# Sharing one block of channels, moving a layer norm to ScalarE and holding back stores in a transformer block on one Trainium2 core

## The chip, the cores and the metric

The kernel runs on one core of one Trainium2 chip. The core has a matrix engine (TensorE, PE in the profile, with its weight loads shown as PEld), a vector engine (VectorE, DVE), an engine for activations (ScalarE, ACT), a general one (GpSimd, POOL) and one that only issues transfers (SyncE, SP). Each takes its instructions in a fixed order. Transfers run on 16 DMA engines. The metric is device time in microseconds (us) of one execution, lower is better.

## The reference

One block on x of 2048 positions and 576 channels, all tensors in bf16:

```
h  = x + A(layernorm(x))          # A: 32 heads of 18 channels; each position attends to 8 positions,
                                  #    2 apart (itself and 7 before it), then a product with wo
h2 = h + B(layernorm(h))          # B: layernorm once more, gelu(y @ w1 + b1) @ w2 + b2, 4608 hidden
```

In A, q, k and v come from one product with wqkv (576 x 1728). Scores are the sum of q times k over the 18 channels, followed by a softmax over the 8 positions. In B the two layer norms in a row are computed as one, with an adjusted epsilon.

## The kernel before, in words

**Tiles.** The positions are cut into 16 tiles j of 128 rows. Position 16p + j is row p of tile j, so the neighbours two apart lie in the same row of tile j - 2, and only the first tiles of each parity need rows shifted by one; these shifted copies of K and V (halos) go through a tensor in DRAM, kv_dram. `store_halo` writes K and V of a tile there, `halo(j, t)` reads one back into the ring buffer kv_ring. There are 15 stores in all. Attention goes over the even tiles from 14 down to 0, then over the odd ones from 15 to 1. `GROUPS` are pairs in that order: (14, 12), (10, 8), (6, 4), (2, 0), (15, 13) and so on. `A` is the same order as a list, so A[0] is tile 14, A[1] tile 12, A[2] tile 10.

**The contraction of 576 rows.** 576 is four and a half times 128. TensorE works here with two half arrays of 64 rows. One bank half (g = 0 or 1) is fed by the upper or the lower 64 rows, and then they swap: `phase(duo, 0, ...)` runs five blocks, `phase(duo, 1, ...)` four, each with two matmuls of 64 rows, so nine in all for each of the two outputs. The product with wqkv uses a fifth block that holds channels 448 to 575, with a swap of blocks 3 and 4 for one of the outputs (`if g == 0 and kt == KF - 1 and sl.start: kt = KF`). The products with wo and w1 use a fifth block that holds channels 512 to 575 twice, once in each half of the partitions. For that, `dma_out` writes the tile's 576 columns and then columns 512 to 575 once more to DRAM, from where a transposing DMA reads the tile back with channels on partitions. `transpose_in` does the same on TensorE, with two more small products when `twice` is set.

**Visits.** The first stage computes q, k and v in 24 visits, numbered 0 to 23. A visit is a set of two or three `duos`; all first phases run, then for each duo the second phase, followed by its eviction (`evac`) and the functions in `between`. Between the phases of a duo a no-operation on GpSimd (`marker`) tells TensorE that a half is free. The table `after` gives what is recorded behind a visit, `loads` which weights are loaded then, `hooks` what TensorE transposes between first and second phases, and `wo_with` puts the output projection of A[0] into visit 17 and that of A[1] into visit 19. The bank "D" serves the transposes and these projections in turn. Three other banks ("C", "A", "B") go round among the q, k, v products.

**LN2.** `ln2_h` adds the projection to x on VectorE. There are two ways from there: `ln2` and `ln2_more` with statistics on VectorE, `ln2_rstd` on GpSimd, `ln2_bias` on VectorE and `ln2_hn` on ScalarE; or `ln2_act` with mean, squares and scale on ScalarE and the root on GpSimd, followed by `ln2_send`. Tiles A[0] and A[1] go the first way.

**Rounds.** After the first stage, round k = 0 to 7 treats the pair GROUPS[k] (w1, gelu, w2) on TensorE, while VectorE does the attention of the next pairs. In the listing c, d are the tiles of GROUPS[k + 1] and e, f those of GROUPS[k + 2]. `m1` and `mid` hold what is recorded with the visits of the product with w1, `ia` and `ib` what is recorded within the products with w2 of the pair's first and second tile. The attention output goes to DRAM by `send_o` and comes back transposed by `read_o`; `wo_duo` uses it. `pending_halo` is the list of stores of K and V not yet made; `halos(n)` makes the next n of them, seven of these in round 1.

**Order.** The program runs under a manual schedule: each engine executes in the order in which the code records, and SyncE's transfers are issued in that order as well. A transfer that waits for something holds up all that SyncE issues behind it. The weight loads also wait for the latest eviction recorded at their place (`pace`).

Of the kernel before, what the change touches and what calls it, by code (L numbers as in the profile page):

```python
# [17 lines left out]
def kernel(  # L18
# [12 lines left out]
    nc = tc.nc  # L31
# [87 lines left out]
    def load_wo(qs):  # L119
        src = A_wo.rearrange("(h d) c -> h d c", h=H)  # L120
        for q in qs:
            load(wo_sb[q * H:(q + 1) * H, :, :], src[:, q:4 * KF:4, :])
            load(woh_sb[q * H:(q + 1) * H, :], src[:, 4 * KF + q % 2, q // 2 * HALF:(q // 2 + 1) * HALF])

    def load_w1h():
        load(b1_bf[:], B_b1.rearrange("(ft p) -> ft p", p=P))
        src = B_w1[KF * P:D, :].rearrange("p (u g c) -> p u g c", u=NU // 3, g=2)
        for r in range(2):
            load(w1h_sb[half_rows(r), :].rearrange("p (u c) -> p u c", u=NU // 3), src[:, :, r, :])

    def load_w1(c):
        cols = slice(c * F // 6, (c + 1) * F // 6)
        load(w1_sb[:, :, cols], B_w1[0:KF * P, cols].rearrange("(k p) c -> p k c", p=P))

    def load_w2(c):
        f0, f1 = (0, 4, 7, 11, 14, 21, FA, FT)[c:c + 2]
        dst = w2a_sb[:, f0:f1, :] if f1 <= FA else w2b_sb[:]
        load(dst, B_w2[f0 * P:f1 * P, :].rearrange("(ft p) c -> p ft c", p=P))
# [38 lines left out]
    def transpose_in(pair, src, twice=True):  # L177
        def turn(rows, kt, c):
            for r in range(2):
                block = src[half_rows(r), c:c + P if rows.start is None else D]  # L180
                nc.tensor.matmul(pair[rows, r, kt * HP:(kt + 1) * HP], lhsT=block, rhs=ident[half_rows(r), half_rows(r)],
                                 start=True, stop=True, skip_group_check=True)

        for kt in range(KT):
            turn(slice(None), kt, min(kt * P, D - P))
        if twice:
            turn(half_rows(0), KF, KF * P)
# [8 lines left out]
    def dma_out(src):  # L196
        td = dram.tile([P, KT * P], BF16, tag="td", name="td", bufs=4)
        nc.sync.dma_start(out=td[:, 0:D], in_=src)
        stored[0] = nc.sync.dma_start(out=td[:, D:KT * P], in_=src[:, KF * P:D]).ins
        return td  # L200
# [5 lines left out]
    def half_rows(r):  # L206
        return slice(r * HP, (r + 1) * HP)

# [51 lines left out]
    def tr_x(j, tag):  # L260
        pair = psum_pair(tag or "CAB"[(ring_pos[0] + 1) % 3], "xt_pt")
        transpose_in(pair, q_all[:, j, :], False)
        if EVEN.index(j) % 2 == 0:
            new_xnT(EVEN[EVEN.index(j):][:2])
        for k0, k1 in ((0, 2), (2, KT)) if j in EVEN[0:2] else ((0, KT),):
            copy = nc.vector.tensor_copy if j == EVEN[1] and k0 == 0 else nc.scalar.copy
            copy(**turned(xnT[j], pair, k0, k1))
# [21 lines left out]
    def store_halo(j, ts=slice(0, 2)):  # L289
        nc.sync.dma_start(out=kv_dram[j, 1:P + 1, ts, :], in_=kv_ring[j % 2][:, j // 2, ts, :])  # L290

    def qkv_duo(j, t):
        def make():
# [3 lines left out]
            def op(g, i, sl, kt):  # L297
                c0 = g * HALF
                if g == 0 and kt == KF - 1 and sl.start:
                    kt = KF  # L300
                return xt[sl, kt, :], (wq_sb[sl, kt, t * D + c0:t * D + c0 + HALF] if kt < KF else wqh_sb[sl, t, c0:c0 + HALF])
# [125 lines left out]

    def read_o(j):
        nc.sync.dma_start_transpose(out=new_oT(j)[:], in_=o_sent.pop(j)[:])
# [3 lines left out]
    def wo_duo(j, tag):  # L433
        def make():
# [3 lines left out]
            def op(g, i, sl, kt):  # L438
                c0 = g * HALF
                return t[sl, kt, :], (wo_sb[sl, kt, c0:c0 + HALF] if kt < KF else woh_sb[sl, :])  # L440
# [29 lines left out]
    def ln2_act(j):  # L470
        h = h_of[j]
        y = sb.tile([P, D], BF16, tag="hn", name="hn", bufs=2)
        nmean, var, rstd = (sb.tile([P, 1], F32, tag=f"ln2_{t}", name=f"ln2_{t}", bufs=2) for t in ("nmean", "var", "rstd"))
        nc.scalar.activation(out=y[:], in_=h[:], func=ACT.Identity, scale=-1.0 / D, accum_out=nmean[:])
        nc.scalar.activation(out=y[:], in_=h[:], func=ACT.Square, bias=nmean[:], accum_out=var[:])
        nc.scalar.activation(out=var[:], in_=var[:], func=ACT.Identity, scale=(1.0 + EPS) / D, bias=eps2[:])
        ins = nc.gpsimd.tensor_tensor(out=rstd[:], in0=var[:], in1=mhalf[:], op=ALU.pow).ins  # L477
        root[0] = ins if j not in GROUPS[1] else None
        hn[j] = (h, rstd, nmean, y)

    def ln2_send(j):
# [3 lines left out]
        hn[j] = dma_out(y[:])  # L485
# [56 lines left out]
    def mlp1_duo(grp, us, tag):  # L542
        def make():
# [5 lines left out]
            def op(g, i, sl, kt):  # L549
                f0 = fts[g][i] * P  # L550
                c0 = (GF * us[i // GF] + i % GF) * P
                return (w1_sb[sl, kt, f0:f0 + P] if kt < KF else w1h_sb[sl, c0:c0 + P]), ht[sl, kt, 0:N]
# [225 lines left out]
    with tc.manual_schedule(engines={ENG.PE, ENG.Activation, ENG.DVE, ENG.SP, ENG.Pool}):  # L778
# [144 lines left out]
        for n, v in enumerate((19, 19, 20, 20, 21, 22)):  # L923
# [18 lines left out]
            17: [c_(ln2, A[0]), c_(att_qk_a, A[2])],  # L942
            18: [c_(ln2_rstd, A[0]), c_(add_b2, A[0]), c_(ln2_bias, A[0]), c_(halo, A[2], 1), c_(att_qk_add, A[2], ((0, 0, 9),))],
# [6 lines left out]
            18: {1: [c_(tr_o, A[1], "D")]},  # L950
            19: [c_(ln2_hn, A[0])],
# [46 lines left out]
        def halos(n):  # L998
            for _ in range(min(n, len(pending_halo))):
                store_halo(pending_halo.pop(0))  # L1000
# [12 lines left out]
        for k, g in enumerate(GROUPS):  # L1013
# [11 lines left out]
            if k == 0:  # L1025
                m1[0] += [c_(halos, 1), c_(load_w2, 6), c_(att_qk_a, d), c_(att_qk_rest, d, 1), c_(halo, d, 1)]
# [7 lines left out]
                ib[8] = [c_(read_o, e), c_(out_store, g[0])]  # L1034
            elif k == 1:
                m1[0] += [c_(pv_sum, d), c_(send_o, d)]
                m1[1] += [c_(att_qk_a, e), c_(halo, e, 1), c_(read_o, d), c_(att_qk_b, e, 0), c_(halos, 7)]
                m1[3] += [c_(att_qk_a, f), c_(halo, f, 1), c_(att_qk_add, f, ((0, 0, 9), (0, 0, 4)))]
# [98 lines left out]
```

## Time and profile before

| | us |
|---|---|
| median of 3 runs | 362.56 (362.54 to 363.0) |
| the profiled execution, its own time | 366.0 |
| span of that execution, first to last instruction | 364.2 |
| first stage (q, k, v), until the first product with w1 | to 67.5 |
| round 0, round 1 (start of w1) | 67.5, 106.2 |
| round 2, 3, 4, 5, 6, 7 (start of w1) | 147.9, 184.4, 220.2, 256.0, 291.8, 327.3 |
| ScalarE busy, VectorE busy, of the span | 235.3, 296.6 |
| DMA, mean over the span | 127 GB/s |

The profile is one execution. Its page gives the busy time of each engine, the granted clock of TensorE, the waits and the costliest groups of instructions by line of the program. In the timeline a row gives the start, the length, the engine, the line, the operation, the tiles written and read, how often, and in brackets the engine's idle time before the row and what ended it. SPq marks SyncE's queue; the length there is that of the issue, not of the transfer.

### The profile page before, as it was taken

Reading aid. Unit: us, or ns where it says so; the run is one execution under the profiler, and the core shown is the slowest. Engines: PE = TensorE matmul, PEld = TensorE weight load, DVE = VectorE, ACT = ScalarE, POOL = GpSimd, SP = SyncE. Lnnn points to the kernel's source line nnn. Section 1 sums busy time; section 2 is a strip of 40 time slices with the busy share of each in tenths; the row PEclk is TensorE's granted clock in tenths of the full one; section 3 lists DMA queues with packets and bytes.
Section 4 is the critical chain, followed back from the end, with each engine's and each line's share of the span. In section 5 each row is a group of like instructions: output and inputs, shape, how many; then the busy total and the mean of one; then the engine's idle time right before and its main releaser. Section 6 shows DMA issues by size and latency. Waiting matters only on the chain.

```text
span 364.2 us, 11562 instructions
## 1 busy us (share of the span) xinstructions
PE 355.0 (97%) x4942; PEld 292.8 (80%) x4942; DVE 296.6 (81%) x417; ACT 235.3 (65%) x521; POOL 45.5 (13%) x61
## 2 busy tenths in 40 slices
PE   7999999999999799999999999999999999999996
PEld 3778977887789777887788778877887788778874
DVE  5999999999989889994799989989998998520431
ACT  4879756897637782468846956695669566805630
POOL 2240004000112010100020102020202020210000
PEclk9999999999999989999999999999999999999999
DMA  7986799963447584651283466344545354263001
GB/s 247 329 278 191 197 218 306 373 227 72 143 90 110 174 207 71 114 90 39 74 121 81 62 133 93 90 98 122 86 88 65 93 85 58 52 120 51 4 1 32
DMA packets 62980, 46.29 MB, mean 127 GB/s; under 512 B 32192, under 2 KB 60736, under 8 KB 62928
## 3 DMA queue, kind: packets, MB, share of 16 engines
q1 hardware_dynamic: 58960, 41.50, 43.2%
q0 software_dynamic: 3744, 3.84, 9.9%
q8 instruction: 38, 0.62, 0.7%
q10 hardware_dynamic: 224, 0.22, 0.2%
q14 instruction: 14, 0.11, 0.1%
HBM read 23.38 MB, written 12.42 MB: 98 GB/s over the span
## 4 chain that ended last, share of the span: by engine, by line
PE 79%; DVE 11%; DMA 6%; ACT 2%; issue 1%; POOL 0%; ACTq 0%; SPq 0%; POOLq 0%
PE pm L216 33%; PE po L664 25%; PE po L576 9%; PE pq L216 7%; PE pw L216 4%; DVE ln_stats L148 2%; DMA x_all<-in_A_x_dram 2%; DMA oT<-td 2%; DVE prod L393 1%; DMA xnT<-xd 1%; DVE prod L399 1%; DVE prod L347 1%; ACT h_all L557 1%; DVE ln_mv L149 1%; DVE prod L338 1%
## 5 line engine op out<-in xcount | busy, mean ns | idle before, releaser
L216 PE MATMUL pm<-hnT,w_sb 64*128 64x256 bf16 x2304 | 143.0, 269 | 0.0
L557 ACT ACTIVATE h_all<-pm,b_sb 128x256 f16<-128x256 f32 (+1 forms) x288 | 108.6, 496 | 51.0 <-PE pm L216 50.4
L216 PEld LDWEIGHTS <-w_sb 64*128 64x128 bf16 x2304 | 113.5, 94 | 13.4 <-issue 1.7
L664 PEld LDWEIGHTS <-h_all 128*128 128x128 f16 x480 | 46.2, 98 | 13.7 <-issue 1.6
L216 PE MATMUL pq<-wq_sb,xnT 64*128 64x288 bf16 x720 | 54.7, 283 | 1.1 <-ACT kv_ring L306 0.4
L216 PEld LDWEIGHTS <-xnT 64*128 64x128 bf16 x864 | 44.0, 94 | 9.9 <-issue 0.8
L347 DVE TENSOR_TENSOR prod<-prod 128x2304 bf16<-128x2304 bf16 (+1 forms) x64 | 44.2, 691 | 2.0
L338 DVE TENSOR_TENSOR prod<-kv_ring,q_all 128x4608 bf16<-128x4608 bf16 x16 | 40.9, 2556 | 3.2 <-POOL ln_rstd L477 2.5
L393 DVE TENSOR_TENSOR prod<-kv_ring,probs 128x4608 bf16<-128x4608 bf16 x16 | 40.9, 2558 | 0.8 <-DMA kv_ring<-kv_dram 0.3
L216 PE MATMUL pm<-hnT,w1h_sb 64*128 64x256 bf16 x288 | 39.5, 269 | 0.0
L664 PE MATMUL po<-w2a_sb,h_all 128*128 128x288 bf16 (+1 forms) x262 | 35.8, 286 | 0.0
L576 PEld LDWEIGHTS <-h_all 128*128 128x128 bf16 x288 | 28.3, 99 | 8.7 <-issue 1.2
L399 DVE TENSOR_TENSOR prod<-prod 128x2304 bf16<-128x2304 bf16 (+1 forms) x32 | 33.9, 1058 | 1.1
L664 PEld LDWEIGHTS <-kv_ring 128*128 128x128 f16 x252 | 24.6, 98 | 6.3
L576 PE MATMUL po<-w2a_sb,h_all 128*128 128x288 bf16 x224 | 29.6, 293 | 0.0
L216 PE MATMUL pq<-wqh_sb,xnT 64*128 64x288 bf16 x144 | 27.6, 283 | 0.0
L766 POOL DMA_DIRECT2D x_all<-o_sb x12 | 10.7, 890 | 126.1 <-PE pw L216 72.2
L216 PE MATMUL pw<-wo_sb,oT 64*128 64x288 bf16 x256 | 20.1, 288 | 2.4 <-DMA oT<-td 2.3
L644 DVE TENSOR_TENSOR kv_ring<-h_all 128x1536 f16<-128x1536 f16 (+3 forms) x9 | 6.8, 760 | 16.1 <-ACT h_all L557 16.1
L664 PE MATMUL po<-w2b_sb,h_all 128*128 128x288 bf16 (+1 forms) x122 | 19.7, 286 | 0.1
L216 PEld LDWEIGHTS <-oT 64*128 64x128 bf16 x288 | 13.8, 95 | 7.0 <-DMA oT<-td 3.3
L161 POOL TENSOR_TENSOR ln_rstd<-ln_veps,mhalf 128x1 f32<-128x1 f32 (+2 forms) x14 | 13.3, 964 | 48.5 <-DVE ln_veps L155 31.7
(107 smaller groups left out, 394.9 us busy)
## 6 DMA issues: line engine op xcount, KB each, us to landing
w_sb<-in_B_w_dram SPq DMA_DIRECT2D x6, 768.0 KB, 5.8
kv_ring<-kv_dram SPq DMA_DIRECT2D x28, 144.0 KB, 2.3
kv_dram<-kv_ring SPq DMA_DIRECT2D x13, 288.0 KB, 3.9
x_all<-in_B_b_dram SPq DMA_DIRECT2D x15, 144.0 KB, 3.7
w2a_sb<-in_B_w_dram SPq DMA_DIRECT2D x2, 1008.0 KB, 7.4
td<-q_all SPq DMA_DIRECT2D x14, 144.0 KB, 1.8
td<-hn SPq DMA_DIRECT2D x14, 144.0 KB, 1.8
x_all<-h POOLq DMA_DIRECT2D x14, 144.0 KB, 4.6
```

Source lines behind the costliest of these rows:

```text
L148: nc.vector.bn_stats(out=stats[:, i, c, :], in_=src[:, c * HALF:(c + 1) * HALF])
L161: nc.gpsimd.tensor_tensor(out=rstd[:], in0=veps[:], in1=mhalf[:].to_broadcast([P, n]), op=ALU.pow)
L216: last = nc.tensor.matmul(duo["g"][r ^ swap][i], lhsT=lhsT, rhs=rhs, start=(swap == 0 and i == 0 and kt == 0), stop=(swap == 1 and kt == K ...
L338: ins = nc.vector.tensor_tensor(out=prod[:], in0=k_ring[j % 2], in1=q_all[:, j, :].unsqueeze(1) .to_broadcast([P, W, D]), op=ALU.mult).ins
L347: nc.vector.tensor_tensor(out=prod[:, :, o * H:o * H + n], in0=prod[:, :, a * H:a * H + n], in1=prod[:, :, c * H:c * H + n], op=ALU.add)
L393: nc.vector.tensor_tensor(out=prod[:].rearrange("p w (d h) -> p w d h", h=H), in0=v_ring[j % 2].rearrange("p w (d h) -> p w d h", h=H), in ...
L399: nc.vector.tensor_tensor(out=prod[:, 0:n, :], in0=prod[:, 0:n, :], in1=prod[:, n:2 * n, :], op=ALU.add)
L557: pace[0] = nc.scalar.activation(out=hT(grp)[:, f, 0:N], in_=ps[:, r, i * N:(i + 1) * N], func=ACT.Gelu_apprx_tanh, bias=b1_sb[:, f:f + 1] ...
L576: nc.tensor.matmul(banks[half], lhsT=hT(grp)[:, f, i * P:(i + 1) * P], rhs=w2_rows(f)[:, half * HALF:(half + 1) * HALF], start=(f == 0), s ...
L644: nc.vector.tensor_tensor(out=s_slot(t, m0, m1), in0=a, in1=b, op=alu)
L664: nc.tensor.matmul(bank, lhsT=l, rhs=r, start=start, stop=stop, skip_group_check=True)
L766: nc.gpsimd.dma_start(out=x_of(j), in_=o_of.pop(j), accum_op=ALU.add)
```

## The change

Three things are changed.

*Shared channels.* The fifth block of o, of wo, of LN2's output and of w1 now holds channels 448 to 575, as that of wqkv does. The swap of blocks is put into a function `block`. `dma_out` writes columns 0 to 511 and then 448 to 575; `transpose_in` loses the `twice` products. The loads of wo and w1 are rearranged to match, and with them the number of transfers; the first six loads of w2 become four.

*LN2 of A[0].* It goes the ScalarE way, in three pieces: `ln2_mean` behind visit 17, `ln2_root` behind the first eviction of visit 18, `ln2_norm` behind the first eviction of visit 19.

*Transfers of rounds 0 and 1.* The output store of GROUPS[0][0] moves from round 0's second product with w2 to behind the seven stores of K and V in round 1. The load of V for d is recorded behind the store of o of d. Stores of K and V made after a read of o wait until the latest such read has landed.

```diff
 def load_wo(qs):
-            load(wo_sb[q * H:(q + 1) * H, :, :], src[:, q:4 * KF:4, :])
-            load(woh_sb[q * H:(q + 1) * H, :], src[:, 4 * KF + q % 2, q // 2 * HALF:(q // 2 + 1) * HALF])
+            rows, k = slice(q * H, (q + 1) * H), KF - q // 2
+            load(wo_sb[rows, 0:k, :], src[:, q:4 * k:4, :])
+            if q >= 2:
+                load(wo_sb[rows, k, 0:HALF], src[:, q + 4 * k + 2, 0:HALF])
+                load(wo_sb[rows, k, HALF:D], src[:, q + 4 * k, HALF:D])
+            load(woh_sb[rows, :], src[:, 4 * KF - 2 + q, q // 2 * HALF:(q // 2 + 1) * HALF])
 def load_w1(c):
-        load(w1_sb[:, :, cols], B_w1[0:KF * P, cols].rearrange("(k p) c -> p k c", p=P))
+        n = KF - 1 if c % 2 == 0 else KF
+        load(w1_sb[:, 0:n, cols], B_w1[0:n * P, cols].rearrange("(k p) c -> p k c", p=P))
+        for r in range(2 * (KF - n)):
+            load(w1_sb[half_rows(r), n, cols], B_w1[n * P + 2 * r * HP:n * P + 2 * r * HP + HP, cols])
 def load_w2(c):
-        f0, f1 = (0, 4, 7, 11, 14, 21, FA, FT)[c:c + 2]
+        f0, f1 = (0, 7, 14, 21, FA, FT)[c:c + 2]
 def dma_out(src):
-        nc.sync.dma_start(out=td[:, 0:D], in_=src)
-        stored[0] = nc.sync.dma_start(out=td[:, D:KT * P], in_=src[:, KF * P:D]).ins
+        nc.sync.dma_start(out=td[:, 0:KF * P], in_=src[:, 0:KF * P])
+        stored[0] = nc.sync.dma_start(out=td[:, KF * P:KT * P], in_=src[:, D - P:D]).ins
+    def block(g, sl, kt):
+        return KF if g == 0 and sl.start and kt == KF - 1 else kt
 def read_o(j):
-        nc.sync.dma_start_transpose(out=new_oT(j)[:], in_=o_sent.pop(j)[:])
+        o_read[0] = nc.sync.dma_start_transpose(out=new_oT(j)[:], in_=o_sent.pop(j)[:]).ins
+    def ln2_mean(j):
...
         nc.scalar.activation(out=y[:], in_=h[:], func=ACT.Identity, scale=-1.0 / D, accum_out=nmean[:])
+        hn[j] = (h, rstd, nmean, y, var)
+    def ln2_root(j):
+        h, rstd, nmean, y, var = hn[j]
         nc.scalar.activation(out=y[:], in_=h[:], func=ACT.Square, bias=nmean[:], accum_out=var[:])
         nc.scalar.activation(out=var[:], in_=var[:], func=ACT.Identity, scale=(1.0 + EPS) / D, bias=eps2[:])
         ins = nc.gpsimd.tensor_tensor(out=rstd[:], in0=var[:], in1=mhalf[:], op=ALU.pow).ins
+    def ln2_norm(j):
         h, rstd, nmean, y = hn[j]
         nc.scalar.activation(out=nmean[:], in_=nmean[:], func=ACT.Identity, scale=rstd[:])
         ln_apply_act(y[:], h[:], rstd[:], nmean[:])
+        hn[j] = y
 after, between
-            17: [c_(ln2, A[0]), c_(att_qk_a, A[2])],
-            18: [c_(ln2_rstd, A[0]), c_(add_b2, A[0]), c_(ln2_bias, A[0]), c_(halo, A[2], 1), c_(att_qk_add, A[2], ((0, 0, 9),))],
+            17: [c_(ln2_h, A[0]), c_(ln2_mean, A[0]), c_(att_qk_a, A[2])],
+            18: [c_(add_b2, A[0]), c_(halo, A[2], 1), c_(att_qk_add, A[2], ((0, 0, 9),))],
-            18: {1: [c_(tr_o, A[1], "D")]},
-            19: [c_(ln2_hn, A[0])],
+            18: {0: [c_(ln2_root, A[0])], 1: [c_(tr_o, A[1], "D")]},
+            19: [c_(ln2_norm, A[0])],
 def halos(n):
-                store_halo(pending_halo.pop(0))
+                ins = store_halo(pending_halo.pop(0))
+                if o_read[0] is not None:
+                    tc.add_manual_dep(ins, o_read[0].name, sync_dep, reason="stores behind the read of o")
 k == 0
-                ib[8] = [c_(read_o, e), c_(out_store, g[0])]
+                ib[8] = [c_(read_o, e)]
 k == 1
-                m1[0] += [c_(pv_sum, d), c_(send_o, d)]
+                m1[0] += [c_(att_pv_sum, d), c_(send_o, d), c_(halo, d, 2)]
-                m1[3] += [c_(att_qk_a, f), c_(halo, f, 1), c_(att_qk_add, f, ((0, 0, 9), (0, 0, 4)))]
+                m1[3] += [c_(out_store, GROUPS[0][0]), c_(att_qk_a, f), c_(halo, f, 1), c_(att_qk_add, f, ((0, 0, 9), (0, 0, 4)))]
```

## The prediction

> **What bounds the kernel now.** First the busy shares, then TensorE's (PE's) waits, then the timeline around the longest.
>
> ```profile
> PE 355.0 (97%) x4942; PEld 292.8 (80%) x4942; DVE 296.6 (81%) x417; ACT 235.3 (65%) x521; POOL 45.5 (13%) x61
> ```
>
> PE is at work almost throughout, so an edit gains only by taking out PE instructions or PE idle time, and loses wherever it makes PE wait. PE's waits for others after the first 15 us are few, and one is large:
>
> ```profile
> PE pw L216 <- DMA oT<-td: 2.3, 2, 2.2
> ```
>
> ```profile
> 123.85 0.67 PE L216 MATMUL pw<-wo_sb,oT 64*128 64x288 bf16 x8
> ...
> 126.80 0.66 PE L216 MATMUL pw<-wo_sb,oT 64*128 64x288 bf16 x8 [2.15 <-DMA oT<-td]
> ```
>
> This is the output projection of d in round k = 1: PE stands 2.15 us for the transposed o. What follows it in the windows of 2 us (PE busy, then PEld, DVE, ACT, POOL, granted clock, DMA share, GB/s):
>
> ```profile
> 126.00:128.00 2.00, 1.20 (x20) 0.98 (x22) 0.94 (x2) 0.81 (x3) 0.00 (x0) 0.98 0.86 326
> 128.00:130.00 2.00, 2.00 (x15) 1.00 (x12) 1.65 (x3) 1.02 (x3) 0.00 (x0) 0.50 1.03 387
> 130.00:132.00 2.00, 2.00 (x13) 1.34 (x12) 1.80 (x5) 1.94 (x6) 0.56 (x1) 0.67 0.86 165
> 132.00:134.00 2.00, 2.00 (x19) 1.61 (x17) 1.97 (x3) 1.93 (x6) 0.57 (x1) 1.00 0.98 75
> ```
>
> The clock fell to half from about 127.9 to 131.3 (0.02 x 2 + 0.50 x 2 + 0.33 x 2 = 1.7 us lost). So the place holds 2.15 + 1.7 = 3.85 us. Why o is late stands in SyncE's queue (start, length of the issue):
>
> ```profile
> 115.02 1.21 SPq L429 DMA_TRANSPOSE oT<-td  x1
> 116.27 0.58 SPq L769 DMA_DIRECT2D out_dram<-x_all  x1
> 116.90 0.43 SPq L333 DMA_DIRECT2D kv_ring<-kv_dram  x1
> 117.42 0.40 SPq L198 DMA_DIRECT2D td<-q_all  x1
> ...
> 122.19 1.21 SPq L429 DMA_TRANSPOSE oT<-td  x1
> 123.45 4.80 SPq L290 DMA_DIRECT2D kv_dram<-kv_ring  x7
> ```
>
> VectorE (DVE) has o at 115.6, but an output store and a V load are issued ahead of its store (117.42), that store shares the engines with them, and the read starts at 122.19. Then seven stores of 288 KB run beside the read, which takes 4.56 us in the chain of waits where its like at 88.67 took 2.87.
>
> **The change, part by part.**
>
> *Order and wait around the read of o.* The output store moves behind the seven stores and the V load behind the store of o. The store of o goes out right after the earlier read's issue, 115.02 + 1.21 = 116.25, some 1.15 us sooner, with 144 KB fewer in front. The page gives a store of o 1.8 us to landing as a median, and the one just before took 115.02 - 110.34 = 4.7 us from its issue to its read. So the read is issued between 118.5 (behind the load of K that waits for DVE's product, ended at 118.2) and 121, and lands 2.9 to 4.0 later: 121.4 to 125. PE asks at 124.64 plus whatever it has lost before. I take no wait: -2.15, bounds -2.15 and -1.8. The seven stores now wait for the landing, 122 to 125 against an issue at 123.45. Behind them on SyncE stand two output stores, two broadcasts of b2 and the stores of hn, at 133.95. Seven issues last 4.8 us, so even from 125 they end at 129.8, and the cover is 4 us. Nobody is late.
>
> The clock loss of 1.7 goes with the idle time in this execution. Whether the timed runs had it is not seen: their median, 362.56, is 1.6 below the span of 364.2, and the profiled execution itself took 366.0. I take half, -0.85, bounds 0 and -1.7. TensorE: Matmul & The Clock Gate (section "Why this matters for your kernels") of the Trainium skill asks only for no idle gap above about 3 us. By it a wait of 2.15 would cost no clock and the term would be 0, but the row above shows half clock after 2.15; the page's window that runs free of the program (its Part 1) would explain that the same wait costs clock in one execution and not in another.
>
> *First LN2 on ScalarE (ACT).* DVE loses two statistics (0.82), one aggregate (0.21), one scale (0.15) and one bias (0.15), 1.3 us, but it does not wait less for it: the next addition of b2 waits for b2's load (0.27 idle at 57.49). What counts is ACT's in-order queue. In the built program the first pass (mean) stands ahead of visit 18's two evictions, square and scale between these, and the copy of the transposed o of A[1] behind them. Before:
>
> ```profile
> 53.16 1.19 ACT L306 ACTIVATE kv_ring<-pq 128x576 bf16<-128x576 f32 x2 [1.82 <-PE pq L216]
> 54.24 0.70 ACT L420 CAST oT<-o_pt 128x640 bf16<-128x640 f32 x1
> ```
>
> ```profile
> 52.72 0.75 DVE L457 TENSOR_TENSOR h<-pw,x_all 128x576 f32<-128x576 f32 x1
> ```
>
> ```profile
> 55.16 0.65 PE L216 MATMUL pw<-wo_sb,oT 64*128 64x288 bf16 x8
> ```
>
> The copy ended at 54.94, PE wanted it at 55.16: cover 0.2 us. The same ACT passes later, for another tile, give the price:
>
> ```profile
> 94.85 0.68 ACT L474 ACTIVATE hn<-h 128x576 bf16<-128x576 f32 x1 [1.18 <-DVE h L457]
> 95.44 0.19 ACT L474 ACTIVATION_READ_ACCUMULATOR hn<-h 128x1 f32 x1
> 95.66 0.78 ACT L475 ACTIVATE hn<-h,ln_nmean 128x576 bf16<-128x576 f32 x1
> 96.34 0.19 ACT L475 ACTIVATION_READ_ACCUMULATOR hn<-h,ln_nmean 128x1 f32 x1
> 96.56 0.29 ACT L476 ACTIVATE ln_var<-ln_var,eps 128x1 f32<-128x1 f32 x1
> ```
>
> Mean 95.66 - 94.85 = 0.81; square to scale 96.85 - 95.66 = 1.19. After: h ends at 53.47, mean to 54.3, first eviction (0.55) to 54.85, square and scale to 56.05, second eviction to 56.6, copy (0.70) to 57.3. PE's Wo of visit 19 starts at 57.35 instead of 55.16: +2.2. The root on GpSimd waits for 56.05, and visit 19's markers queue behind it there, but their readers now come after 57.9. Part of it comes back: PE's idle 0.20 before 59.81 (for ACT's eviction, late behind ln2_hn) and 0.16 before 61.66 (a marker behind the second root) fall into the shift, and so does 0.16 before 84.60. -0.5. Bounds of the edit: 0 (if h came 2 us earlier, which nothing in DVE's queue offers) and +3.1 (next item).
>
> *Shared channels.* The number of matmuls is the same; each of four PE transposes loses 2 of 12 products. Twelve take 0.47, so 0.08 each; two lie under the waits of visits 18 and 19, two on the path: -0.16. The stores of o split 512 + 128 columns instead of 576 + 64: 0, the smaller one landed 0.2 us after the larger. W1 takes six more issues and Wo four, of 0.45 on SyncE. Wo's four stand ahead of the V load at 44.10 and the transpose at 46.09. The load's data queue behind 0.9 MB issued from 39.27 on, so I take 0 for it, at worst 2 x 0.45 = +0.9. The transpose feeds visit 18 with no cover (PE waited 0.15 for it at 51.23), at worst 4 x 0.45 = 1.8, all inside the 2.2 that visit 19 loses anyway. W2 takes two issues fewer, in front of nothing that waits: 0.
>
> **Sum.** +2.2 - 0.5 - 0.16 = +1.5 up to PE's 123.85; then -2.15 and -0.85: -1.5. From 362.56: **361.1**. Against the profiled execution, where the clock loss is whole: 364.2 + 1.5 - 3.85 = 361.9 of span. PE then runs 0.6 to 2.4 us earlier than now; DVE has 5.0 us idle at 169.16 for PE, so it follows.
>
> **Rivals.** (A, forecast) as summed; with the clock term at its ends 361.9 to 360.2. (B) The LN2 work hides on ACT, which is idle 35%: then only gains are left, -0.16 - 2.15 - 0.85, 359.4, with the whole clock loss 358.5. Against it: the cover of 0.2 us and the in-order queue. (C) The gains cancel: without the profiler's traffic the read of o takes not 4.56 but nearer 2.87, the wait of 2.15 shrinks towards 0.45 and costs no clock. At 1.5 the sum is 0, 362.6. For it: timed runs are shorter than the profile; against it: the late issue at 122.19 has its cause in DVE and SyncE's order. In this case the stores' wait does nothing, because PE already arrives 1.5 us later. (D, the other side) Visit 19's wait itself costs a window of half clock: 2.2 + 0.9 (V load late) - 0.66 + 1.7 = +4.1, less 2.15: +2.0, **364.5**. It decides from an idle time between 1.7 us (the sum between 5 and 16.6 at the start, clock kept at 1.00 throughout) and 2.15 in one piece (clock lost). Visit 19's stands in between or above.
>
> **Numbers.** A 0.46, B 0.10, C 0.17, D 0.27. A change of 0.2%, 0.73 us, is what a measurement of this kernel can tell from none. Of A 0.38 is faster by more and 0.08 within; B is faster; of C 0.15 is within and 0.02 slower; D is slower. Faster 0.48, within 0.23, slower 0.29. Range 359.4 (B with half the clock) to 364.4 (D's edge); A's own 360.2 to 361.9.
>
> **What would show it.** Right: an idle time of about 2 us before Wo in visit 19, ended by ACT's copy of o; no wait for oT before Wo near 126; full clock after it. Wrong: a copy of o by 55.3 (B); an oT wait that is still there; half clock near 58 to 61 (D); a transpose of x landing past 53, when visit 18 adds more than I count.

## The result and the profile after

The changed kernel takes 365.06 us (median of six runs, 364.42 to 365.66), the kernel before 362.62 us (362.48 to 363.0) beside it: a ratio of 1.0069, 95% interval 1.0057 to 1.0081. It is slower by 0.7%, 2.4 us, where 1.5 us less was forecast.

The first thing to compare is not the two profiles but each profile with its own runs. The profiled execution of after is an ordinary one: span 363.5, time 365.3. The profiled execution of before is not: it took 366.0 us, the six others 362.5 to 363.0. So the two profiles say that the change gains 0.7 us, and the runs that it loses 2.4. The kernel before ran 100 more times beside the experiments below, at 361.11 to 364.83 us (median 362.3): none of these came near 366.0 either.

Busy time, part 1 of the page of after:

```profile
PE 352.1 (97%) x4934; PEld 294.5 (81%) x4934; DVE 295.1 (81%) x412; ACT 237.1 (65%) x527; POOL 44.1 (12%) x61
```

The PE waits for others from 40 to 130 us of after (sum, times, longest):

```profile
PE pq L221 <- DMA xnT<-xd: 1.8, 1, 1.8
PE pw L221 <- ACT oT L424: 1.1, 1, 1.1
PE pm L221 <- DMA hnT<-td: 0.7, 1, 0.7
PE pq L221 <- POOLq L231: 0.6, 1, 0.6
PE pw L221 <- DMA oT<-td: 0.3, 1, 0.3
```

The one large wait of before, for o in round 1, is gone, and five others stand in its place. On PE's timeline three of them lie between 51 and 65 us (start, length, operation, and in brackets the idle time before it with what ended it):

```profile
53.02 0.66 PE L221 MATMUL pq<-wq_sb,xnT 64*128 64x288 bf16 x8 [1.75 <-DMA xnT<-xd]
...
57.85 0.66 PE L221 MATMUL pw<-wo_sb,oT 64*128 64x288 bf16 x8 [1.08 <-ACT oT L424]
...
64.25 0.66 PE L221 MATMUL pq<-wq_sb,xnT 64*128 64x288 bf16 x7 [0.57 <-POOLq L231]
```

The first is visit 18 waiting for the third transposing read of x. SyncE's queue shows why (start and length of the issues), first in before, then in after:

```profile
45.01 0.42 SPq L104 DMA_DIRECT2D woh_sb<-in_A_wo_dram  x1
46.09 1.32 SPq L280 DMA_TRANSPOSE xnT<-xd  x1
...
52.11 1.33 SPq L280 DMA_TRANSPOSE xnT<-xd  x1
53.57 0.50 SPq L104 DMA_DIRECT2D x_all<-in_B_b_dram  x1
```

```profile
43.63 1.35 SPq L104 DMA_DIRECT2D wo_sb<-in_A_wo_dram  x3
45.02 0.42 SPq L104 DMA_DIRECT2D woh_sb<-in_A_wo_dram  x1
45.54 0.37 SPq L337 DMA_DIRECT2D kv_ring<-kv_dram  x1
46.01 1.31 SPq L104 DMA_DIRECT2D wo_sb<-in_A_wo_dram  x3
47.37 0.41 SPq L104 DMA_DIRECT2D woh_sb<-in_A_wo_dram  x1
47.89 1.33 SPq L285 DMA_TRANSPOSE xnT<-xd  x1
...
54.40 1.30 SPq L285 DMA_TRANSPOSE xnT<-xd  x1
55.79 0.52 SPq L104 DMA_DIRECT2D x_all<-in_B_b_dram  x1
```

Eight issues for Wo where there were four: the read goes out at 47.89 instead of 46.09 and lands at 52.97 instead of 51.19, 1.8 us later. The four issues of 0.45 are not the whole account of that, though the sum is the same: in this execution the second read of x already went out 0.49 later (38.42 instead of 37.93), and in before SyncE stood 0.66 us between the last of Wo's issues and the read, where it now stands 0.11. So the change delays the read by some 1.3 us, an estimate from these rows. Behind it everything moves on: the store of the next pair of x, the fourth read that waits for that store's landing (54.40 instead of 52.11), and the load of b2 behind the fourth read (55.79 instead of 53.57, landing at 60.06 instead of 57.47). Who waits for b2 is VectorE; its timeline in before and in after:

```profile
57.49 0.76 DVE L499 TENSOR_TENSOR x_all<-h,x_all 128x576 bf16<-128x576 f32 x1 [0.27 <-DMA x_all<-in_B_b_dram]
```

```profile
53.90 2.55 DVE L342 TENSOR_TENSOR prod<-kv_ring,q_all 128x4608 bf16<-128x4608 bf16 x1
60.16 0.76 DVE L517 TENSOR_TENSOR x_all<-h,x_all 128x576 bf16<-128x576 f32 x1 [3.71 <-DMA x_all<-in_B_b_dram]
```

In before this wait was 0.27 us, that is, VectorE already arrived with b2 and had no cover. Now it stands 3.71 us, and the addition starts 2.7 us later than before. VectorE carries this through round 0: its two waits for others between 62 and 106 us end at 65.26 and 105.30 instead of 62.66 and 102.70, both 2.6 us later. PE pays for it behind there: it waits 0.57 for a GpSimd marker behind the second LN2's root (before: 0.16), then 0.30 for o (before: 0.16) and 0.74 for hn.

The wait of 1.08 us is the predicted one. ScalarE in after:

```profile
54.01 0.69 ACT L484 ACTIVATE hn<-h 128x576 bf16<-128x576 f32 x1 [2.49 <-DVE h L463]
...
55.49 0.77 ACT L489 ACTIVATE hn<-h,ln_nmean 128x576 bf16<-128x576 f32 x1
...
56.38 0.29 ACT L490 ACTIVATE ln_var<-ln_var,eps 128x1 f32<-128x1 f32 x1
56.59 0.63 ACT L310 ACTIVATE kv_ring<-pq 128x576 bf16<-128x576 f32 x1
57.12 0.68 ACT L424 CAST oT<-o_pt 128x640 bf16<-128x640 f32 x1
```

Mean, square and scale stand in front of the copy of o, which ends at 57.80 instead of 54.94.

Round 1 in after. SyncE first, then the windows of 2 us (PE, PEld, DVE, ACT, POOL, granted clock, DMA share, GB/s):

```profile
123.63 1.21 SPq L435 DMA_TRANSPOSE oT<-td  x1
126.40 4.71 SPq L295 DMA_DIRECT2D kv_dram<-kv_ring  x7
```

```profile
126.00:128.00 2.00, 2.00 (x39) 1.93 (x36) 1.97 (x2) 2.00 (x7) 0.00 (x0) 1.00 0.40 151
128.00:130.00 2.00, 2.00 (x29) 1.54 (x26) 1.97 (x4) 2.00 (x7) 0.00 (x0) 1.00 1.02 373
130.00:132.00 2.00, 2.00 (x19) 1.61 (x17) 1.80 (x6) 1.94 (x6) 0.07 (x1) 1.00 0.84 318
```

The seven stores wait for the landing of the read (126.38), PE is busy throughout and the clock full: this part does what it says. The account by PE's phases, from the start of the transposes of o in visit 16 to the first w1 product, from there to the first w1 product of round 1, and from there to that of round 2:

| | visits 16 to 22 | round 0 | round 1 |
|---|---|---|---|
| before, its profile (366.0 us) | 21.25 | 38.71 | 41.70 |
| after, its profile (365.3 us) | 23.16 | 39.45 | 37.74 |
| difference | +1.91 | +0.74 | -3.96 |

1.91 + 0.74 = 2.65 us of loss, near the 2.44 of the runs. The 3.96 of round 1 would then have to be missing from most runs of before, and they are indeed 3.4 us shorter than the profiled execution. What is known of it: its rounds 2 to 7 take what they take in p0_before (below) to within 0.03 us, so the excess lies ahead of them. The half clock is not usual: one such window brings the mean granted clock of an execution to 0.994 or 0.995 (0.994 in this one), and of the 100 further runs of before 91 had 0.998 or more. The profiled execution is 3.4 us above the median of the six and 3.7 above that of the 100; 1.7 of this are clock, which leaves 1.7 to 2.0 for the wait of 2.15. So by this estimate an ordinary execution waits some 0.2 to 0.5 us for o. The wait itself was traced in this one execution only.

### The profile page after: what moved, and what is told of

It is laid out like the page before. It is cut to its first block, busy times and chain, and to the rows that moved or that the text cites. A ratio compares the mean times of both kernels' runs of the same rounds, so it can differ in the third digit from the quotient of the medians.

```text
span 363.5 us, 11555 instructions
## 1 busy us (share of the span) xinstructions
PE 352.1 (97%) x4934; PEld 294.5 (81%) x4934; DVE 295.1 (81%) x412; ACT 237.1 (65%) x527; POOL 44.1 (12%) x61
## 4 chain that ended last, share of the span: by engine, by line
PE 72%; DVE 13%; DMA 6%; ACT 3%; SPq 2%; issue 2%; POOL 0%; POOLq 0%; ACTq 0%
PE pm L221 34%; PE po L682 22%; PE pq L221 7%; PE po L594 5%; PE pw L221 4%; DVE ln_stats L155 2%; DVE prod L351 2%; DMA hnT<-td 2%; DVE prod L397 1%; DMA xnT<-xd 1%; DVE prod L342 1%; DMA x_all<-in_A_x_dram 1%; DVE prod L403 1%; ACT h_all L575 1%; DMA td<-hn 1%
## 5 line engine op out<-in xcount | busy, mean ns | idle before, releaser
L221 PEld LDWEIGHTS <-w_sb 64*128 64x128 bf16 x2304 | 115.2, 94 | 12.7 <-issue 2.2
L221 PEld LDWEIGHTS <-xnT 64*128 64x128 bf16 x864 | 44.8, 94 | 11.3 <-DMA xnT<-xd 2.4
L594 PE MATMUL po<-w2a_sb,h_all 128*128 128x288 bf16 x224 | 28.5, 286 | 0.0
L491 POOL TENSOR_TENSOR ln_rstd<-ln_var,mhalf 128x1 f32<-128x1 f32 x14 | 9.7, 696 | 108.8 <-ACT ln_var L490 108.8
```

The costliest lines, as they stand in the source:

```text
L221: last = nc.tensor.matmul(duo["g"][r ^ swap][i], lhsT=lhsT, rhs=rhs, start=(swap == 0 and i == 0 and kt == 0), stop=(swap == 1 and kt == K ...
L594: nc.tensor.matmul(banks[half], lhsT=hT(grp)[:, f, i * P:(i + 1) * P], rhs=w2_rows(f)[:, half * HALF:(half + 1) * HALF], start=(f == 0), s ...
```

## The experiments

No version with the transposing reads of x, o and hn and only parts of the change was run. In all eighteen kernels below each transposing read is a plain one of the same bytes, in pieces of 256 bytes unless said otherwise:

```diff
-        nc.sync.dma_start_transpose(out=dst, in_=td[:])
+        nc.sync.dma_start(out=dst, in_=td[:].rearrange("a c -> (a c)").rearrange("(k p t) -> p k t", p=P, t=P))
```

What is read comes back unturned, so values differ from the reference in all of them; the instructions on PE, VectorE, ScalarE and GpSimd are the kernel's own. The issue is shorter (0.4 us against 1.2 to 1.3) and the landing sooner (3.4 us against 5.1 for the third read of x), so each series has a base of its own. Ratios are to the kernel before itself, run beside each. "Stretch" is the first column of the table above, from the profile of each; those of s1_after and s4_both hold a window of half clock, worth 1.7 us.

| run | what | us | ratio, 95% | stretch |
|---|---|---|---|---|
| p0_before | before | 361.03 | 0.9969 [0.9952, 0.9986] | 20.84 |
| p1_after | whole change | 362.66 | 1.0027 [1.0008, 1.0045] | 22.09 |
| p2_shared | shared channels alone | 361.42 | 0.9985 [0.9965, 1.0005] | 20.60 |
| p3_ln2 | LN2 on ScalarE alone | 362.93 | 1.0015 [0.9995, 1.0035] | 22.54 |
| p4_transfers | order and wait of round 1 alone | 361.09 | 0.9960 [0.9944, 0.9976] | 20.84 |
| p6_ln2_late | whole, LN2 behind the copy | 361.17 | 0.9966 [0.9943, 0.9988] | 20.80 |
| p7_no_ln2 | whole without LN2 | 361.63 | 0.9973 [0.9955, 0.9990] | 20.59 |
| s0_before | before, slow reads of x | 364.26 | 1.0051 [1.0024, 1.0078] | 21.62 |
| s1_after | whole, slow reads | 365.42 | 1.0071 [1.0046, 1.0097] | 23.84 |
| s2_shared | shared alone, slow reads | 365.19 | 1.0064 [1.0040, 1.0087] | 23.80 |
| s3_wo_early | s1, Wo two visits earlier | 366.02 | 1.0087 [1.0063, 1.0111] | 22.53 |
| s4_both | s3, LN2 behind the copy | 366.07 | 1.0094 [1.0071, 1.0117] | 23.99 |
| m0_before | before, reads 3 and 4 slow | 363.46 | 1.0039 [1.0020, 1.0058] | 21.54 |
| m1_after | whole, reads 3 and 4 slow | 364.78 | 1.0075 [1.0052, 1.0097] | 23.07 |
| m2_wo_hole | m1, Wo behind visit 4 | 365.56 | 1.0082 [1.0052, 1.0111] | 22.44 |
| m3_wo_hole_ln2_late | m2, LN2 behind the copy | 364.87 | 1.0073 [1.0046, 1.0100] | 20.81 |
| m4_ln2_late | m1, LN2 behind the copy | 364.75 | 1.0062 [1.0046, 1.0077] | 23.65 |
| m5_ln2_late_b2_early | m4, b2 ahead of the fourth read | 363.07 | 1.0008 [0.9990, 1.0025] | 22.36 |

**Part by part on fast reads.** The edits are those parts of the diff that the name says.

> The kernel before, with one thing put in place of another: each transposing DMA is a plain DMA of the same bytes in the same 256-byte pieces, so x, o and hn come back untransposed; all order, waits and bytes stay. It is the base for the runs that follow. Theory 1 (the profiled execution of before, 366.0, was an unusual one; timed runs of after lie 1.8 us above their spans, so before's usual span is 360.8): spans of 360 to 361.5, a wait for oT before Wo in round 1 of 0 to 0.8 us, full clock after it. Rival 1 (the wait of 2.15 us and the half clock are in every run): spans near 364, both there.

> The whole change, with the same plain DMAs as the base. If the plain DMAs stand in well, it is slower than the base by 1.5 to 3 us (the change itself: 2.4). Theory 1: PE waits in visits 18 and 19 for 2 to 3 us together, VectorE stands 2 to 4 us for the load of b2 behind visit 18, and round 1 has no wait for oT. Rival 1: equal to the base or faster, as the wait saved in round 1 is as large as the one gained.

> The base with the shared channels alone (loads of wo, w1, w2 included). Theory 1 (the four more issues of Wo hold up what stands behind them on SyncE): the third read of x goes out 1.2 to 1.8 us later, visit 18 waits for it, the load of b2 lands later too: slower than the base by 0.8 to 1.8 us. Rival 2 (the first stage loses by LN2 on ScalarE alone): within 0.4 us of the base.

> The base with LN2 of A[0] on ScalarE alone. Theory 1: Wo of visit 19 waits about 2 us for ScalarE's copy of o, 0.3 to 0.5 comes back: slower than the base by 1.2 to 2 us. Rival 2: the same. Rival 3 (the loss is all in SyncE's queue, ScalarE has room): within 0.4 us of the base, wait before Wo of visit 19 under 0.3.

PE's waits from 40 to 130 us, first of p0_before, then of p1_after:

```profile
PE o_pt L181 <- DVE h L460: 0.2, 1, 0.2
PE pq L219 <- POOLq L229: 0.2, 1, 0.2
```

```profile
PE pw L224 <- ACT oT L427: 1.4, 1, 1.4
PE o_pt L188 <- DVE h L466: 0.5, 1, 0.5
PE pq L224 <- ACT kv_ring L313: 0.4, 1, 0.4
```

p1_after is 1.63 us over p0_before, p3_ln2 1.90: LN2 on ScalarE is enough for that loss, through the wait for the copy of o. The shared channels cost 0.39 us by the medians, within the spread of either, since with a landing after 3.4 us the later issue of the third read still reaches visit 18. And p0_before, with LN2, orders and stores as before, has no wait for o in round 1.

**Is the gain there?**

> Only the order and the wait around the read of o in round 1 (output store behind the seven stores, these behind the landing of the read, the V load behind the store of o), on the plain reads of p0_before; to be read beside p0_before, which stood at 0.9969 of the kernel before. Theory (the wait of 2.15 us and the half clock behind it belong to one unusual execution, so taking their cause away brings nothing in the usual one): within 0.5 us of p0_before, 0.9955 to 0.9985 of the kernel before, no PE wait near 123 us either way. Rival 1 (the prediction: the read of o limits most executions): 1.5 to 3 us below p0_before, 0.989 to 0.993. Rival 2 (the wait for the landing costs, since the stores and all that stands behind them on SyncE come later): 0.5 us or more above p0_before, 0.9985 or more.

> The whole change but for the first LN2, which stays on VectorE; plain reads as in p0_before. Theory (with fast reads LN2's place in ScalarE's queue is the only loss of the change): 0 to 0.5 us over p0_before, 0.9965 to 0.9985 of the kernel before, with no wait for the copy of o before Wo of visit 19. Rival (shared channels and transfers carry a good part of the 1.63 us that the whole change cost in p1_after): 0.8 us or more over p0_before, 0.999 or more.

p4_transfers stands at 0.9960, p0_before at 0.9969, with overlapping intervals; both need 37.74 us for round 1, as do all eighteen kernels within 0.01. Only the profiled execution of before needs 41.70. So on plain reads both rivals fall, the gain of 1.5 to 3 us and a cost of holding the stores back. They do not test the prediction's own case: in p0_before the plain read of o lands 2.42 us after its issue with the seven stores right behind it, where the transposing one took 4.56 in the profile of before and 2.76 in after. That the gain is not there in an ordinary execution rests on the run times and clocks of the kernel before itself, given above. p7_no_ln2 lands at 0.9973: what is left of the change without LN2 costs 0.04% by the ratios, which can't be told from nothing.

**LN2's place.** p6_ln2_late moves three instructions behind the copy:

```diff
-            17: [c_(ln2_h, A[0]), c_(ln2_mean, A[0]), c_(att_qk_a, A[2])],
+            17: [c_(ln2_h, A[0]), c_(att_qk_a, A[2])],
-            18: {0: [c_(ln2_root, A[0])], 1: [c_(tr_o, A[1], "D")]},
+            18: {1: [c_(tr_o, A[1], "D"), c_(ln2_mean, A[0]), c_(ln2_root, A[0])]},
```

> The whole change on the fast plain reads (as p1_after), but the first LN2's mean, square and scale stand behind the copy of the transposed o of A[1] on ScalarE instead of in front of it; read against p1_after and p0_before through the kernel before that runs beside each. Theory (the loss is the place in ScalarE's queue, in front of the copy): the wait of 1.42 us before Wo of visit 19 goes and the time falls by 1.2 to 1.9 us against p1_after, to 360.8 to 361.5, that is 0.9970 to 0.9985 of the kernel before beside it. Rival (the loss is ScalarE's work as such, wherever it stands): the wait moves to the evictions of visits 19 and 20 or to the transposes of hn, and the time stays within 0.5 us of p1_after, 362.2 to 363.2, 1.001 to 1.004 of the kernel before.

0.9966 against p1_after's 1.0027: the loss is gone. It is not hidden altogether. PE's only wait over 0.2 us in the stretch, and GpSimd's root ahead of the marker that ends it:

```profile
57.30 0.66 PE L224 MATMUL pq<-wq_sb,xnT 64*128 64x288 bf16 x7 [1.17 <-POOLq L234]
```

```profile
57.27 1.11 POOL L494 TENSOR_TENSOR ln_rstd<-ln_var,mhalf 128x1 f32<-128x1 f32 x1 [28.83 <-ACT ln_var L493]
```

The marker stands behind the root in GpSimd's queue, and the root waits for ScalarE's scale; PE goes on as the root starts, so it pays for the root's wait and not for its 1.11 us. That the stretch is still as short as p0_before's, 20.80 against 20.84, fits the shorter transposes: see below.

**Slow reads.** To bring the landing of x near the 5.1 us of the transposing read, each read of x is split in two, with pieces of 128 bytes:

```diff
+        xt = new_xnT(ODD[2 * i:2 * i + 2])[:].rearrange("p k (m t) -> p (k m) t", t=HP)
+        src = xd[i][:, :, :].rearrange("j a c -> (j a c)").rearrange("(m p t) -> p m t", p=P, t=HP)
+        for r in range(2):
+            nc.sync.dma_start(out=xt[half_rows(r), :, :], in_=src[half_rows(r), :, :])
```

> The kernel before with plain reads in place of the transposing ones (as in p0_before), but each read of x split into two transfers with pieces of 128 bytes instead of one with 256, so that it takes longer to land, nearer to the 5.1 us that the transposing read took in the trace of before. The read blocks come back untransposed, so the values are not those of the reference. Both theories: as p0_before to within 0.8 us, 360.9 to 361.9, because visit 18 has only some 0.15 to 0.5 us to wait for x; the read of x lands 4 to 6 us after its issue (3.4 in p0_before).

> The whole change on the same slow reads of x; against s0_before. Theory (two separate losses: ScalarE's LN2 in front of the copy of o, some 1.4 to 2 us, and Wo's four extra issues in front of the read of x, hidden by the fast reads but not by slow ones): +2.2 to +3.0 us, as the real change showed (+2.4), with a PE wait of about 1 to 2 us for xnT in visit 18 and what is left of the wait for the copy of o behind it. Rival (LN2 on ScalarE is the whole loss): +1.3 to +1.9, as p1_after had over p0_before (+1.63), with no xnT wait over 0.5 us.

> Only the shared channels (Wo's and w1's loads, the stores of o and hn, the PE transposes) on the slow reads of x; LN2, the order and the wait of round 1 as before; against s0_before. Theory: +0.8 to +2 us, since Wo's four extra issues of some 0.45 us each stand in front of the read of x, with a PE wait of that size for xnT in visit 18. Rival (the extra issues are free): within 0.4 us of s0_before, as p2_shared was of p0_before (+0.39), with no xnT wait over 0.5 us.

s0_before, at 364.26, is slower than either theory gave it: PE waited 0.9 us for the second read of x as well. Against it the whole change costs 1.16 us and the shared channels alone 0.93, with intervals that overlap; the traces say more, with waits for x in visit 18 of 2.13 and 1.20 us. So Wo's issues are not free when the read is slow. But the sum of two separate losses (2.2 to 3.0) is wrong as well: the one wait covers the other. From the transposes of o in visit 16 to Wo in visit 19 PE needs 8.90 us in p0_before; with LN2 on ScalarE it needs 10.82 in p1_after, without a wait for x, 10.83 in m1_after (below) with one of 0.62, and 11.21 in after with one of 1.75. s1_after needs 12.57 with 2.13, but 1.7 of this is a window of half clock behind the wait for x (see the last section), so its short wait of 0.29 for the copy of o can't be set beside the 1.42 of p1_after. The first of ScalarE's passes for LN2 does run there while PE waits for x: it starts at 53.35, PE at 54.23.

> The whole change on the slow reads of x (as s1_after, 1.0071 of the kernel before), with Wo's last two groups of loads issued three and two visits earlier, so that their eight issues no longer stand in front of the third read of x. LN2 on ScalarE stays in front of the copy of o. Theory (the two waits lie one behind the other and the first covers the second): the wait for x in visit 18 falls from 2.13 us to under 0.7, the wait for the copy of o grows from 0.29 to 1 to 1.5 us, and the time hardly moves: 364.6 to 365.6, 1.005 to 1.008. Rival (the issues of Wo are the whole loss with slow reads): the time falls by 1.2 us or more, to s0_before's 1.0051 or below, and the copy's wait stays under 0.5.

> As s3_wo_early, and the first LN2's mean, square and scale moved behind the copy of the transposed o, as in p6_ln2_late. Theory (two waits, either of which is enough for the loss): with both causes gone the loss goes: 363.4 to 364.4, 1.002 to 1.005 of the kernel before, that is s0_before's time or a little less, with no wait over 0.7 us in visits 18 and 19. Rival (a third cause, such as the load of b2 that stands behind the reads of x and holds up VectorE): 365 or more, 1.0065 or more.

In s3_wo_early the wait for x fell to 0.33 and the copy's rose to 1.42, as the theory of overlap has it; the total rose by 0.6 us, beyond the 365.6 given. s4_both did not lose its loss: x was 2.02 us late again, with the third read issued at 48.73. These two edits were bad ones. Issued earlier, Wo's loads stand ahead of the store of the same x, and the read waits for that store. They show only that the time stays up with either wait; s4_both also has half clock behind its wait for x.

**Only the third and fourth read slow.** The same split for these two, which gives a base whose second read is as early as in before; then Wo's last two groups behind visit 4, where SyncE waits for VectorE.

```diff
-        for q, v in enumerate((6, 8, 11, 12)):
-            loads[v] = [c_(load_wo, [q])]
+        for q, v in enumerate((6, 8, 4, 4)):
+            loads[v] = loads.get(v, []) + [c_(load_wo, [q])]
```

> The kernel before with plain reads as in p0_before, but the third and fourth read of x (those that feed visits 18 and 21) split into two transfers with pieces of 128 bytes, so that they land some 5 us after their issue as the transposing read did (5.1 us for the third). Read blocks come back untransposed, so values are not those of the reference. Both theories: between p0_before and s0_before, 0.997 to 1.003 of the kernel before; visit 18 waits under 0.5 us for x.

> The whole change on the reads of m0_before. Theory (two causes, Wo's issues ahead of the third read and LN2 ahead of the copy of o, each worth 1 to 2 us, that overlap in part): 1.6 to 2.8 us over m0_before (the real change: +2.44), with a wait for x in visit 18 of 0.8 to 2 us and for the copy of o of 0.3 to 1.4. Rival (LN2 alone): +1.3 to +1.7 and no wait for x over 0.5 us.

> As m1_after, with Wo's last two groups of loads (eight issues) put behind visit 4, where SyncE stands for some 4 us waiting for VectorE (23.84 to 28.13 us in the trace of after), so that none of them is in front of the third read of x. Theory (overlap): the third read is issued 1.5 us or more earlier, its wait goes, the copy's wait rises to 1.1 to 1.5, and the time falls by 0.3 to 1.2 us against m1_after, staying 1 us or more over m0_before. Rival 1 (Wo's issues are the whole of it with reads this slow): falls to m0_before's time within 0.5 us. Rival 2 (they are free): within 0.3 us of m1_after.

> As m2_wo_hole, with the first LN2's mean, square and scale behind the copy of the transposed o. Theory (no third cause): within 0.5 us of m0_before or below it, since eight issues, of which four were there before the change, are out of the way of the third read; 0.995 to 1.003 of the kernel before. Rival (a third cause, b2's load and VectorE behind it): 0.8 us or more over m0_before.

The whole change costs 1.3 us here (1.0075 against 1.0039, intervals that overlap by a little), less than the 1.6 expected: 0.62 us of waiting for x, 1.42 for the copy, 0.86 for a marker. By the time, m2 and m3 gain nothing; by the stretch m2 is 0.63 shorter than m1, and m3 is 20.81, below m0's 21.54. What they win there they lose at 36 us, where PE waits 0.54 (m2) and 2.88 us (m3) for the first read of x, which the moved loads delay. With both causes gone the loss of visits 16 to 22 is gone, but PE begins that stretch at 50.47 us in m3 and at 46.23 in m1, so the transfers had 4 us more; that it was the two causes is not shown here. A free place for Wo's issues was not found.

**The load of b2.** m4 is m1 with LN2 behind the copy; m5 has b2's load ahead of the fourth read of x as well.

```diff
-            14: [c_(att_pv, A[1]), c_(in_x, 3), c_(load, b2_bc, B_b2.partition_broadcast(P))],
+            14: [c_(att_pv, A[1]), c_(load, b2_bc, B_b2.partition_broadcast(P)), c_(in_x, 3)],
```

> As m1_after (the whole change; third and fourth read of x slow), with the first LN2's mean, square and scale behind the copy of the transposed o, Wo's loads where the change has them. Theory (LN2's place is the largest of three causes, b2's late load the next): no wait for the copy of o, the wait for x in visit 18 at 0.6 us, a wait of 0.6 to 1.2 us for a GpSimd marker in visit 21; 0.6 to 1.4 us under m1_after, 1.003 to 1.006 of the kernel before. Rival (something else sets the end of the stretch, so that the wait only moves): within 0.4 us of m1_after's 1.0075.

> As m4_ln2_late, with b2's load issued ahead of the fourth read of x instead of behind it. Theory: b2 lands 2 us or more before 58, VectorE does not wait for it, the marker's wait falls below 0.3 us, and the time falls by another 0.4 to 1 us, to 0.1 to 0.6 us round m0_before: 1.001 to 1.005 of the kernel before. Rival (b2's wait has cover): VectorE waits less, but PE not, within 0.3 us of m4_ln2_late.

VectorE's addition of b2, in m4_ln2_late and in m5_ln2_late_b2_early:

```profile
53.27 2.55 DVE L349 TENSOR_TENSOR prod<-kv_ring,q_all 128x4608 bf16<-128x4608 bf16 x1
60.14 0.76 DVE L524 TENSOR_TENSOR x_all<-h,x_all 128x576 bf16<-128x576 f32 x1 [4.32 <-DMA x_all<-in_B_b_dram]
```

```profile
53.82 2.55 DVE L349 TENSOR_TENSOR prod<-kv_ring,q_all 128x4608 bf16<-128x4608 bf16 x1
56.69 0.76 DVE L524 TENSOR_TENSOR x_all<-h,x_all 128x576 bf16<-128x576 f32 x1 [0.32 <-DMA x_all<-in_B_b_dram]
```

PE's waits of the two, in the same order:

```profile
PE pq L224 <- POOLq L234: 2.0, 2, 1.2
PE pq L224 <- DMA xnT<-xd: 1.7, 1, 1.7
```

```profile
PE pq L224 <- DMA xnT<-xd: 1.3, 1, 1.3
PE pq L224 <- POOLq L234: 1.2, 1, 1.2
```

m4 is level with m1 (364.75 and 364.78), so the rival holds there: with slow reads LN2's place alone is not what sets the end. The profiles of the two differ in one thing more: the third read, issued at 46.17 in m4 and 46.16 in m1, lets PE go on at 52.51 and 51.58. m5 falls by 1.7 us to 363.07, more than the 0.4 to 1 expected: b2 lands at 56.60 instead of 60.05. Of the two waits for markers in m4 the one of 0.80 us goes, the one behind LN2's root (1.17) stays, and x is late in both. The traces show 1.29 us of it in the stretch and 0.20 in round 0; 0.80 is the marker's, and 0.39 is a shorter wait for x (1.66 and 1.27), which the edit does not explain. The whole change with these two edits, at 1.0008, is level with the kernel before and 0.3% under its own base, with intervals that overlap by a little. It was not run with the transposing reads, so whether it beats the kernel before there is open.

## Why the prediction was wrong

**The step that failed is the gain.** "I take no wait: -2.15, bounds -2.15 and -1.8" and "I take half, -0.85" took 3.0 us out of runs that had next to nothing of the kind to lose; the forecast missed by 3.9. The wait for o in round 1, as long as this, and the half clock behind it belong to the one profiled execution: by the estimate above an ordinary one waits some 0.2 to 0.5 us, at full clock. The figures stood in one sentence of the prediction: that execution took 366.0 and the median was 362.56. They are 3.4 us apart, and wait and clock loss together are 3.85; the two were not set against each other. The bounds should have been -2.15 and 0 for the wait, with the end near 0 the likelier. Rival C had the right mechanism ("the wait of 2.15 shrinks towards 0.45 and costs no clock") at a chance of 0.17, and still left 1.5 us of gain in it.

**Visit 19: right.** Start 57.35 instead of 55.16 was forecast, +2.2. After has 57.85; less 0.43 us by which this execution was later since visit 16 began (the other profiles lie as far apart there, with and without the change), that is +2.26. It came in two pieces, 1.75 for x and 1.08 for o, and the sentence that a late x would lie "all inside the 2.2 that visit 19 loses anyway" held up to that point. That the size is ScalarE's queue and not luck is shown by p3_ln2: without any wait for x it needs 10.83 us from visit 16 to this point, 1.93 more than p0_before.

**Wo's four issues taken as 0: wrong, but not in visit 18.** The step asked who waits for the third read, and stopped there. Behind the third read on SyncE come a store, the fourth read and the load of b2, and VectorE had 0.27 us of wait for b2 already. The prediction quoted that 0.27 as a reason why VectorE would not be faster, and didn't ask what it would be when b2 came later. PE's waits for the marker, o and hn grew by 0.57 - 0.16 + 0.30 - 0.16 + 0.74 = 1.29 us, where the prediction had the first two fall to nothing as part of its -0.5. At the first Wo product of round 1 PE is 126.93 - 123.85 - 0.43 = 2.65 late, where +1.5 was forecast. m5 against m4 shows the link from b2 to the marker by itself, on slow reads; that o and hn are late by it too is read from VectorE's 2.6 us in after.

**Shorter transposes: right in sign, too small.** -0.08 each was worked out as 2 of 12 products. On PE's timeline a transpose of o in before, and one in after:

```profile
53.52 0.47 PE L181 MATMUL o_pt<-ident,q_all 64*128 64x64 bf16 x12
53.92 0.66 PE L216 MATMUL pq<-wq_sb,xnT 64*128 64x288 bf16 x8
```

```profile
55.23 0.31 PE L188 MATMUL o_pt<-ident,q_all 64*128 64x64 bf16 x10
55.38 0.65 PE L221 MATMUL pq<-wq_sb,xnT 64*128 64x288 bf16 x8
```

0.40 from start to start against 0.15: the last two products cost 0.25, three times their share. The four make 0.9 to 1.0 us. That is why waits of 3.40 us between 51 and 65 us, against 0.51 in before (0.15, 0.20 and 0.16), lengthen the stretch by 1.91 only, and why p7_no_ln2 has the shortest stretch of all.

**Order and wait of round 1: right as to the trace** (no wait for oT, full clock, stores at 126.40 and nobody late), and worth nothing. **Rival D**, a half clock for visit 19's wait, did not occur in the profile of after (five of its six runs had a mean granted clock of 0.999 or 1.0); it came near the measured time (364.5) by a cause that wasn't there. **Rival B**, LN2 hidden on ScalarE, is refuted by p3_ln2 at the place that the change gives it; p6_ln2_late comes near it at another.

What stays open is the split of the real 2.4 us between LN2's place and Wo's issues. The stand-ins give 1.6 to 1.9 us for the first with fast reads and 0.9, within the intervals, for the second with slow ones, and show that the waits overlap; parts of the change on the transposing reads themselves were not tried.

## What to carry to other kernels

Before a wait in a profile is counted as a gain, compare the profiled execution's own time with the runs: if it is longer by about the size of the wait, the wait may be that execution's alone, and the gain's lower bound is 0. The mean granted clock of the runs tells in the same way whether a window of half clock is usual. When an issue is added to an in-order queue, follow all that stands behind it to the first reader without cover, not only the next transfer; an engine that waits 0.3 us for a load today has no cover at all. Two causes that act in the same stretch are not added: take each away alone and both together, and read the stretch beside the total, since an edit can pay for its gain somewhere else.

## What the runs showed of the hardware

The clock fell to half for one window of 3.41 us after idle times that were well shorter than the window. PE and windows of s1_after around its wait for x:

```profile
54.23 0.66 PE L224 MATMUL pq<-wq_sb,xnT 64*128 64x288 bf16 x7 [2.13 <-DMA xnT<-xd]
```

```profile
54.00:56.00 2.00, 1.77 (x22) 1.31 (x24) 1.78 (x1) 0.13 (x2) 0.00 (x0) 0.77 0.40 148
56.00:58.00 2.00, 2.00 (x28) 1.42 (x24) 0.00 (x0) 0.98 (x2) 0.00 (x0) 0.50 0.77 126
58.00:60.00 2.00, 1.71 (x26) 1.19 (x23) 0.00 (x0) 1.84 (x5) 0.56 (x1) 0.88 0.86 170
```

From 30 us on the profiles hold four such cases: idle times of 2.02 (s4_both), 2.13 (s1_after), 2.15 (the profile of before) and 2.88 us (m3_wo_hole_ln2_late) were each followed by one window at half clock; 1.66, 1.75 and 1.79 us (m4_ln2_late, after, s2_shared) were not. TensorE: Matmul & The Clock Gate of the Trainium skill (section "Why this matters for your kernels") asks for no idle gap above about 3 us; here 2.0 us were enough, and cost 1.7 us more (0.23 x 2 + 0.50 x 2 + 0.12 x 2 in s1_after). In the first 12 us, where PE also does small transposes, the window ahead of one at half clock held 1.31, 1.49 and 1.97 us of idle time in pieces (s0_before, s3_wo_early, p6_ln2_late), but 1.45 in the profile of before and 1.41 in s4_both passed at full clock. So there neither the longest gap nor their sum decides alone, and what does is open.
